# A stored instruction order for the second part of an attention and mixture-of-experts kernel, and two subtractions on another engine

## The chip, the cores and the metric

The kernel runs on one core of a Trainium2 chip. The metric is the device time of one execution in microseconds (us). A core has TensorE (PE: matmuls; PEld: its weight loads), VectorE (DVE), ScalarE (ACT), GpSimd (POOL) and SyncE (SP, which issues most DMAs). Each engine works through its own instructions in the order in which they stand in its queue, and waits on semaphores for the others.

## What is computed

Attention with four sink positions and a window of 128, and behind it a mixture of eight experts of which each token takes two. The random inputs are float32. Cut from the reference:

```python
keep = (pos[None, :] < 4) | ((rel >= 0) & (rel < 128))       # 4 batches, 8 heads, 768 positions, 64 wide
x = softmax(where(keep, q @ k.T / 8, -1e9)) @ v              # as 3072 tokens x 512
logits = x @ w_gate + log1p(exp(x @ w_noise)) * noise        # 3072 x 8
top2, top2_w = two largest of each row, softmax of the two
for e in range(8):
    for k in range(2):
        mask = top2[:, k] == e
        out[mask] += top2_w[mask, k, None] * (relu(x[mask] @ w1[e]) @ w2[e])   # 512 -> 1024 -> 512
```

## The kernel before

**Two parts.** The first part (to about 165 us of the profiled execution) is the attention, the routing of the first three batches and the start of expert 0; its order is a table, `ORDER`, carried out by `Plan.in_order`. The second part (`phase_two`) has the routing of the last batch and the experts. Both are written as a plan: `Plan.op` and `Plan.dma` record operations with an engine, a modelled duration, a priority and the keys that they read and write; nothing is issued until the plan is run. The second part is run by `Plan.run` (L1871: `p2.run()`), a list scheduler: at each step, of the operations that are ready on an engine by modelled times, it takes the one with the smallest priority. The order of each engine's queue follows from these model times. The constants of the model are `P2`.

**Routing of the last batch.** ScalarE and VectorE make the noisy logits, VectorE finds the two largest (L854, L858), their one-hot rows `oh` (L865) and their sum `m` (L867). TensorE ranks the tokens of each expert (`rank`, L875 to L881), VectorE makes factors from the ranks (L912 to L936; L936 multiplies last), TensorE places token numbers into the table of slots (`place`, L946), and VectorE makes the gather indices (`idg`, L970; `rt_idi`, L986). Indirect DMAs on GpSimd then fetch tokens: L1050 for the rest of expert 0, L1067 for the later experts, whose rows go by way of a DRAM buffer `x_sorted` (stores L1072, loads L1076 into `xg`, all issued by SP).

**Experts.** An expert has six or seven tiles of up to 128 tokens. Matrices are split into a high and a low half (`hi` on ScalarE, `lo` as a subtraction, L374 `minus`), and a product takes three matmuls. Expert 0 goes up (L1118 to L1120) and down (L1389 to L1391) in two pieces. Experts 1 to 7 go up by seven products of quarter matrices, named a to g, per pair of columns (L1519 to L1521, 6 matmuls each); several products add into the same accumulator bank, so ScalarE copies a bank out (`kept`, L1534) and VectorE adds (`added`, L1537) before the next product may write there; then ScalarE and VectorE make the two halves of the hidden rows (L1540, L1543). Each tile goes down by eight groups of three 512-column matmuls (a down product: L1550; the half tile L1553). ScalarE scales the sum (L1398), and GpSimd scatters it into the output with an adding indirect DMA (L1413). The last tile of all is added up on VectorE (L1431) to what a fetch brought, and stored (L1436).

**Buffers that tie the queues.** Weight chunks are loaded into two buffers `st` (L1181) and split from there (L1190, L1231, L374, L1239); rows into two `xg`, transposed on VectorE (L1273), which also takes the weights of the tokens from them (L1321, L1324), then split (L1287, L374); scaled sums have three buffers (laid in `turned` and `tmp`), each free when the scatter from it has landed; the banks of the products b and d have one buffer each.

**Two weight chunks of expert 0** (the last of w1, the third of w2; `w_chunk`, L1173) have their low half made by GpSimd:

```python
        if not q:
            w_chunk(plan, nc, c, sh, w1, w2, 0, 1, 3, -60, "Pool")
            w_chunk(plan, nc, c, sh, w1, w2, 0, 2, 2, -50, "Pool")
```

Of the kernel before, what the change touches and what calls it, by code (L numbers as in the profile page):

```python
# [76 lines left out]
)  # L77
ZERO = (0,) * 16
EACH = (0,) * 48
CAP = 832  # L80
# [5 lines left out]
ZEROS = 16  # L86
WIDE = 416
P2 = dict(sg=.01, ga=-57.86, gs=4.26, wt=-28.03, x=-83.35, xs=13.55, wa=-27.67, ws=27.26, w2=-33.31, w2s=11.84, wb=1.97,
          slack=0.55, sums=0.55, lands=3.2, late=0.93, gather=1.27, pair=5.89, a=1.92, b=7.67, d=7.57, c=-0.02,
          e=-5.07, f=-4.27, g=3.49)  # L90


# [4 lines left out]
PORT = 9  # L97
# [4 lines left out]
class Plan:  # L102
# [67 lines left out]
    def in_order(self, order, idle=None):  # L170


        n, ops = len(self.ops), self.ops
        left, succ = [len(o[4]) for o in ops], [[] for _ in ops]
        for i, o in enumerate(ops):
            for d in o[4]:
                succ[d].append(i)
        rows = {e: list(x) for e, x in order.items()}
        rows["DMA"] = [i + 1 for i in rows["SP"] if i + 1 < n and ops[i + 1][0] == "DMA"]
        assert sorted(sum(rows.values(), [])) == list(range(n))  # L180
        at, start, ptr = [self.low] * n, [0.0] * n, dict.fromkeys(rows, 0)
        free = {e: self.begin.get(e, self.low) for e in rows}
        kind, port = 0, self.low
        fill = []
        for _ in range(n):
            t, e = min((max(at[x[ptr[e]]], free[e], port if ops[x[ptr[e]]][6] == PORT else self.low), e)
                       for e, x in rows.items() if ptr[e] < len(x) and not left[x[ptr[e]]])
            i = rows[e][ptr[e]]
            ptr[e] += 1
            d = ops[i][1]  # L190
            if ops[i][6] == PORT:
                port = t + d
            start[i] = t
            if e == "PE":
                if idle and t < idle[0]:
                    w = max(free[e], idle[1])
                    fill += [w] * int((t - w) / (idle[2] * (2 if t < self.cold else 1)))
                d = (d + (SWITCH.get(kind, .1) if ops[i][6] != kind else 0)) * (2 if t < self.cold else 1)
                kind = ops[i][6]
            free[e] = end = t + d  # L200
            for s in succ[i]:
                lat = ops[i][5]
                if isinstance(lat, tuple):
                    lat = lat[e != ops[s][0]]
                if lat is None:
                    lat = SELF.get(e, .06) if e == ops[s][0] else self.LAT.get((e, ops[s][0]), .2)
                at[s] = max(at[s], end + lat)
                left[s] -= 1
        self.start, self.free = start, free
        for _, _, fn in sorted([(start[i], i, o[3]) for i, o in enumerate(ops) if o[3]] + [(t, -1, idle[3]) for t in fill], key=lambda x: x[:2]):  # L210
            fn()
        return max(free.values())
# [575 lines left out]
def routing(nc, plan, cst, sh, b, t0, nt, z, xbuf):  # L788
# [5 lines left out]
    last = T0 + nt == sh.T  # L794
    c, get = cst, plan.get
    gid = b
# [12 lines left out]
    def t(name):  # L809
        if name in ("oh", "z", "r2"):  # L810
            return (name, gid)
        if last and name in ys:
            return ("y", ys[name])
        if name == "lg":
            return ("lg", b)
        tag = "rt_" + name
        plan.rings.setdefault(tag, 1)
        return (tag, gid)
# [44 lines left out]
    pair = [128, 2, nt]  # L863
# [31 lines left out]
        for q in range(DM // 128):  # L895
            nc.sync.dma_start(dram(xbuf, (T0 + 1) * 128 * sh.XW + q * sh.SW + 128, [[sh.XW, 128], [128 * sh.XW, nt], [1, E]]), rt("w"))

    plan.dma(z if last else plan.now, keep, 1.2, r=[t("w")], w=[("wrow", gid)], u=[("old", 0)] * last, n=12)
    most = c["most"]
    ends = last or T0 + nt == sh.T - NT  # L900
    tab = lambda nm: c[nm].rearrange("p e t -> p (e t)")[:, fl]
    if ends:
        i = int(last)
# [137 lines left out]
def gather(plan, nc, cst, sh, xbuf, e, t, z, after=None):  # L1041


    n = sh.first[e] + t
# [8 lines left out]

    if not e:
        kept = [("xrow", n) for n in range(sh.NA // 256 * (sh.H // 2))] + [("wrow", b) for b in range(sh.B - 1)] + [("blank", 0)]
        plan.op("Pool", 1.28, z, go, r=[("idg", int(not first))] + kept * first, w=[row], lat=5.4 if first else 4)
        return
    m = n - sh.first[1]
    rows = cst["xsort"][m]
# [19 lines left out]
    if after:  # L1079
        key, src, region = after  # L1080
        held = [("held", n)]
        plan.op("Pool", .12, zs, lambda: nc.gpsimd.tensor_copy(cst["spacer"], src()), r=[key], w=held, u=[region], lat=0)  # L1082
    plan.op("Pool", P2["gather"], zs, sort, r=[("rt_idi", sh.B - 1)] + held + [("xe", f) for f in range(sh.F // 128)] * (m == 2), w=[sg], lat=P2["lands"])
    plan.dma(zs, store, 1.6, r=[sg], w=[("xs", n)], late=0)
    plan.dma(z, load, 1.4, r=[("xs", n)], w=[row], late=.5)

# [251 lines left out]
def experts(tc, plan, cst, sh, w1, w2, xbuf, out):  # L1338
# [122 lines left out]
    for q, (e, tiles, width) in enumerate(info):  # L1461
# [4 lines left out]
                weight(plan, nc, c, sh, e, t, -100 + (t - FA) * 7)  # L1466
                rows_turn(plan, nc, c, sh, e, t, size(e, t), "TX", -100 + (t - FA) * 7)
        if not q:
            w_chunk(plan, nc, c, sh, w1, w2, 0, 1, 3, -60, "Pool")
            w_chunk(plan, nc, c, sh, w1, w2, 0, 2, 2, -50, "Pool")  # L1470
        order = [t for t in tiles if size(e, t) == 128]
        order[1:1] = [t for t in tiles if size(e, t) != 128]
        for t in order:
# [334 lines left out]
def moe_kernel(ctx, tc, sh, qk_t, v, vsink, w_gates, noise, w1c, w2c, w1, w2, out):  # L1808
# [14 lines left out]
    with ExitStack() as both:  # L1823
# [44 lines left out]
        for i in range(int(late / .22)):  # L1868
            p2.op("PE", .22, -1000, lambda: ones(p2.get("Y", 0, [128, sh.DM], F32, "ps")))
        phase_two(tc, nc, p2, cst, sh, w1c, w2c, xbuf, out)  # L1870
        p2.run()  # L1871
    spill(tc, cst, sh, w1, w2, xbuf, out)


# [21 lines left out]
```

## Time and profile before

| | |
|---|---|
| Time, median of 3 runs | 717.66 us (717.14 to 718.05) |
| Time of the profiled execution | 718.88 us |
| Its span | 717.2 us, 13573 instructions |
| TensorE busy | 692.4 us (97%), 4755 matmuls |
| VectorE, ScalarE, GpSimd busy | 530.8 us (74%), 403.6 us (56%), 281.4 us (39%) |
| TensorE's granted clock | 0.9 or more of full in all 40 slices |
| Data moved by DMA | 123.41 MB, 172 GB/s on the mean |
| Chain that ended last, by engine | PE 74%, DMA 9%, DVE 5%, ACT 3%, issue 3%, POOL 3% |

The profile is that of one execution. Its span is what the instructions cover, its time has the start and end of the launch as well. The busy share says how much of the span an engine had an instruction in work; a matmul's end is modelled. An idle time in brackets in a row of the timeline is that of the engine just before that instruction, and behind the arrow stands what ended it. Lines are those of the kernel before.

### The profile page before, as it was taken

How to read it: one execution, taken by the hardware profiler on the slowest of the kernel's cores; microseconds unless marked ns; L12 is line 12 of the kernel's file. 1: busy time of each engine (PE TensorE's matmuls, PEld its weight loads, DVE VectorE, ACT ScalarE, POOL GpSimd, SP SyncE). 2: the span in 40 equal slices, each digit the busy share in tenths (PEclk: the TensorE clock that was granted, in tenths of full speed). 3: DMA queues.
4: the chain of work that ended last, by engine and by line, in shares of the span. 5: the costliest groups of instructions: out<-in, count | busy, mean ns of one | idle time of the engine just before them, and what ended most of it. 6: DMA issues, size and time to landing. Idle time of an engine off the chain costs nothing.

```text
span 717.2 us, 13573 instructions
## 1 busy us (share of the span) xinstructions
PE 692.4 (97%) x4755; PEld 586.5 (82%) x4755; DVE 530.8 (74%) x1279; ACT 403.6 (56%) x1115; POOL 281.4 (39%) x383
## 2 busy tenths in 40 slices
PE   8999999998999999998999999999999999999995
PEld 4777777766878889878988998898899889889984
DVE  7899988968526977957796769587877968775620
ACT  6998989763115545635564655355555555645430
POOL 3435575683227432552253316330732530181022
PEclk9999999999999999999999999999999999999999
DMA  7775787575479997566548655854576390264132
GB/s 252 218 259 163 240 272 200 139 200 183 153 244 228 319 286 232 103 156 197 177 95 205 172 153 131 209 161 140 129 229 201 90 253 32 89 121 100 59 45 46
DMA packets 87336, 123.41 MB, mean 172 GB/s; under 512 B 18656, under 2 KB 55392, under 8 KB 87264
## 3 DMA queue, kind: packets, MB, share of 16 engines
q1 hardware_dynamic: 75856, 94.64, 42.4%
q0 software_dynamic: 11408, 27.86, 19.4%
q8 instruction: 38, 0.62, 0.4%
q14 instruction: 34, 0.28, 0.1%
HBM read 81.75 MB, written 40.73 MB: 171 GB/s over the span
## 4 chain that ended last, share of the span: by engine, by line
PE 74%; DMA 9%; DVE 5%; ACT 3%; issue 3%; POOL 3%; SPq 0%; POOLq 0%; DVEq 0%; ACTq 0%
PE Y L1550 31%; PE B L1519 9%; PE B L1520 9%; PE B L1521 9%; PE S L468 3%; DMA xg<-x_sorted 3%; ACT cbuf L489 2%; DMA x_rows<-strip 2%; PE B L550 2%; DMA sg<-x_rows,idg 2%; PE Y L1553 2%; PE B L525 1%; DMA vn<-in_v 1%; PE B L553 1%; DMA xg<-x_rows,idg 1%
## 5 line engine op out<-in xcount | busy, mean ns | idle before, releaser
L1413 POOL DMA_INDIRECT out<-tmp,idx x34 | 87.1, 2562 | 153.3 <-ACT tmp L1398 149.1
L1520 PE MATMUL B<-x,wr 128*128 128x384 f32 (+1 forms) x392 | 134.7, 344 | 0.0
L1550 PE MATMUL Y<-w2a,hb 128*128 128x512 f32 x504 | 128.9, 395 | 0.0
L1550 PE MATMUL Y<-w2b,hb 128*128 128x512 f32 x504 | 124.8, 392 | 0.0
L1550 PEld LDWEIGHTS Y<-w2b,hb 128*128 128x128 f32 x504 | 94.5, 188 | 20.1
L1550 PEld LDWEIGHTS Y<-w2a,hb 128*128 128x128 f32 x504 | 94.2, 188 | 19.5
L1519 PE MATMUL B<-xe,wr 128*128 128x384 f32 (+1 forms) x224 | 77.2, 345 | 3.5 <-ACT tmp L1534 2.2
L1521 PE MATMUL B<-xe,wr 128*128 128x384 f32 (+1 forms) x224 | 76.8, 343 | 0.1
L1520 PEld LDWEIGHTS B<-x,wr 128*128 128x128 f32 x392 | 73.6, 188 | 2.5
L374 DVE TENSOR_TENSOR wr<-st,wr 128x512 fp32r<-128x512 f32 (+1 forms) x86 | 59.4, 695 | 13.3 <-ACT wr L1231 13.1
L489 ACT ACTIVATE cbuf<-S,nb 128x132 f32<-128x132 f32 x192 | 68.4, 372 | 0.9
L1231 ACT ACTIVATE wr<-st 128x512 fp32r<-128x512 f32 x84 | 52.2, 624 | 12.6 <-DVE st L374 9.8
L1519 PE MATMUL B<-x,wr 128*128 128x384 f32 (+1 forms) x168 | 57.9, 345 | 1.3 <-ACT tmp L1534 1.3
L1521 PE MATMUL B<-x,wr 128*128 128x384 f32 (+1 forms) x168 | 57.7, 343 | 0.9 <-DVE wr L374 0.9
L1082 POOL COPY spacer<-hb 1x1 f32<-1x1 f32 x38 | 12.3, 324 | 96.1 <-ACT hb L1540 88.2
L1519 PEld LDWEIGHTS B<-xe,wr 128*128 128x128 f32 x224 | 42.0, 188 | 7.3 <-ACT tmp L1534 3.1
L1398 ACT ACTIVATE tmp<-Y,wc 128x512 f32<-128x512 f32 x31 | 21.2, 688 | 46.8 <-PE Y L1550 32.7
L1413 POOL DMA_INDIRECT out<-turned,idx x17 | 31.9, 1876 | 36.9 <-ACT turned L1398 33.8
L1534 ACT ACTIVATE tmp<-B 128x384 f32<-128x384 f32 (+1 forms) x56 | 27.7, 499 | 32.3 <-PE B L1521 27.8
L1540 ACT ACTIVATE hb<-B 128x384 fp32r<-128x384 f32 (+1 forms) x56 | 28.0, 502 | 27.9 <-DVE B L1537 13.3
L468 PE MATMUL S<-kq 64*64 64x196 f32 (+2 forms) x768 | 40.9, 325 | 2.3 <-ACT cbuf L489 1.0
L1521 PEld LDWEIGHTS B<-xe,wr 128*128 128x128 f32 x224 | 42.0, 188 | 0.6 <-DVE wr L374 0.4
(314 smaller groups left out, 1553.6 us busy)
## 6 DMA issues: line engine op xcount, KB each, us to landing
st<-in_w1c SPq DMA_DIRECT2D x32, 512.0 KB
st<-in_w2c SPq DMA_DIRECT2D x32, 512.0 KB
kq<-in_qk_t SPq DMA_DIRECT2D x15, 780.0 KB
xg<-x_sorted SPq DMA_DIRECT2D x42, 272.0 KB
x_sorted<-sg SPq DMA_DIRECT2D x30, 272.0 KB
out<-zt SPq DMA_DIRECT2D x31, 256.0 KB
vn<-in_v SPq DMA_DIRECT2D x16, 384.0 KB
x_rows<-strip SPq DMA_DIRECT2D x48, 128.0 KB
```

Source lines behind the costliest of these rows:

```text
L374: eng.tensor_tensor(out, a, b, op=OP.subtract)
L468: nc.tensor.matmul(whole[x, h, c0:c1], kq(g)[r, KS + 128 * j + 64 * s:KS + 128 * j + 64 * s + 64], kq(g)[r, o + c0:o + c1], start=True, st ...
L489: nc.scalar.activation(C(n)[:, u], S_(n, 0, KW)[:, u // 2, u % 2], AF.Exp, scale=1.0 / math.sqrt(D), bias=get("nb", n)[:, u // 2, u % 2:u ...
L1231: plan.op("ACT", .03 + .255 * m, z, lambda: nc.scalar.activation(h(), src(), AF.Copy), r=[st], w=[(*key, b)] + old, u=[key, ex], lat=P2["s ...
L1398: nc.scalar.activation(get("y", Y[e, t], [128, DM]), get("Y", Y[e, t]), AF.Copy, scale=c["wc"][e % 2][:, t:t + 1])
L1413: d = nc.gpsimd.indirect_dma_start(out=out, out_offset=bass.IndirectOffsetOnAxis(ap=c["idx"][:size(e, t), e, t:t + 1], axis=0), in_=get("y ...
L1519: nc.tensor.matmul(p, wh, h, start=start and not k, stop=False, skip_group_check=True)
L1520: nc.tensor.matmul(p, wh, l, start=False, stop=False, skip_group_check=True)
L1521: nc.tensor.matmul(p, wl, h, start=False, stop=k == 1, skip_group_check=True)
L1534: nc.scalar.activation(u_of(e, k), src(), AF.Copy)
L1540: nc.scalar.activation(hx(e, f, 0, j), src(), AF.Relu)
L1550: nc.tensor.matmul(p, h[:, x * (CAP + R) + 128 * t:x * (CAP + R) + 128 * t + 128], w[:, y], start=(f == 0 and x + y == 0), stop=(f == FC - ...
```

## The change

The second part is no longer scheduled by `Plan.run`. A new table, `ORDER2`, holds for each engine the numbers of the plan's operations in the order in which they are to be issued, 688 for TensorE, 868 for VectorE and 520 for ScalarE, and `Plan.in_order` issues them so. The same operations are there, with the same tiles. `in_order` learns to place operations of the first part that the second reads (their engine is a tuple). The two subtractions of expert 0 go to VectorE. Some modelled times and reads change (a gather now names the rows of weights of the last batch among what it reads); the stored order, not these times, now sets each engine's queue.

```diff
+ORDER2 = dict(
+    PE=(15, 12, 13, 16, 11, 95, 96, 97, 14, 98, 103, 104, 105, 106, 33, 111, 112, 113, 114, 119, 163, 120, 121, 193,
...
-          slack=0.55, sums=0.55, lands=3.2, late=0.93, gather=1.27, pair=5.89, a=1.92, b=7.67, d=7.57, c=-0.02,
+          slack=0.25, sums=0.25, lands=3.2, late=0.93, gather=1.27, pair=5.89, a=1.92, b=7.67, d=7.57, c=-0.02,
...
+        rows.update({o[0]: [i] for i, o in enumerate(ops) if isinstance(o[0], tuple)})
...
-    plan.dma(z if last else plan.now, keep, 1.2, r=[t("w")], w=[("wrow", gid)], u=[("old", 0)] * last, n=12)
+    plan.dma(z if last else plan.now, keep, 1.2, r=[t("w")], w=[("wrow", gid)], u=[("old", 0)] * last, n=5 if last else 12)
...
-        plan.op("Pool", 1.28, z, go, r=[("idg", int(not first))] + kept * first, w=[row], lat=5.4 if first else 4)
+        plan.op("Pool", 1.28, z, go, r=[("idg", int(not first))] + (kept if first else [("wrow", sh.B - 1)]), w=[row], lat=5.4 if first else 4)
...
-        plan.op("Pool", .12, zs, lambda: nc.gpsimd.tensor_copy(cst["spacer"], src()), r=[key], w=held, u=[region], lat=0)
-    plan.op("Pool", P2["gather"], zs, sort, r=[("rt_idi", sh.B - 1)] + held + [("xe", f) for f in range(sh.F // 128)] * (m == 2), w=[sg], lat=P2["lands"])
+        plan.op("Pool", .7, zs, lambda: nc.gpsimd.tensor_copy(cst["spacer"], src()), r=[key], w=held, u=[region], lat=0)
+    plan.op("Pool", P2["gather"], zs, sort, r=[("rt_idi", sh.B - 1), ("wrow", sh.B - 1)] + held + [("xe", f) for f in range(sh.F // 128)] * (m == 2), w=[sg], lat=P2["lands"])
...
-            w_chunk(plan, nc, c, sh, w1, w2, 0, 1, 3, -60, "Pool")
-            w_chunk(plan, nc, c, sh, w1, w2, 0, 2, 2, -50, "Pool")
+            w_chunk(plan, nc, c, sh, w1, w2, 0, 1, 3, -60)
+            w_chunk(plan, nc, c, sh, w1, w2, 0, 2, 2, -50)
...
-        p2.run()
+        p2.in_order(ORDER2)
```

Three places show what moves. A row has the line, the operation, the tile written and, behind the arrow, those read. Lines of the changed kernel are 127 or 128 higher (L995 is L867 of before).

VectorE at the routing of the last batch, before: `m` is L867, `hb` the low half of expert 0's hidden rows, `oh` the one-hot rows.

```order
L854 MAX turned_152<-turned_152 128x8 x6
L1378 SCALAR_TENSOR_TENSOR hb_2996<-B2_78,hb_2996 128x512
L858 MAX_INDEX turned_152<-turned_152 128x8 x6
L865 TENSOR_TENSOR oh3_131<-io_94,turned_152 128x96
L888 RECIPROCAL z3_132<-turned_152 128x6
L867 TENSOR_TENSOR m_114<-oh3_131 128x48
L1378 SCALAR_TENSOR_TENSOR hb_2996<-B0_76,hb_2996 128x512
L912 COPY turned_152<-B3_79 128x8
```

The same place in the changed kernel:

```order
L982 MAX turned_152<-turned_152 128x8 x6
L986 MAX_INDEX turned_152<-turned_152 128x8 x6
L993 TENSOR_TENSOR oh3_131<-io_94,turned_152 128x96
L995 TENSOR_TENSOR m_114<-oh3_131 128x48
L1016 RECIPROCAL z3_132<-turned_152 128x6
L1506 SCALAR_TENSOR_TENSOR hb_3001<-B2_78,hb_3001 128x512
L1506 SCALAR_TENSOR_TENSOR hb_3001<-B0_76,hb_3001 128x512
L1045 TENSOR_TENSOR turned_152<-oh3_131,B3_79 128x96
```

The split of the hidden rows (L1378, now L1506) that stood between the maxima and their indices now stands behind `m`, beside the second one; `m` comes ahead of the reciprocal (L888, now L1016).

ScalarE around the first products of expert 2, before: L1190 splits weights, L1398 scales a sum for the scatter, the first L1534 copies out product a of expert 2.

```order
L1287 ACTIVATE x7_3455<-turned_152 128x4x32
L1287 ACTIVATE x7_3455<-turned_152 128x2x32
L1190 ACTIVATE w2a_4385<-st_4294 128x1024
L1398 ACTIVATE tmp_2956<-Y_4364,wc1_151 128x512
L1190 ACTIVATE w2a_4421<-st_4382 128x1024
L1534 ACTIVATE tmp_2956<-B2_78 128x416
L1540 ACTIVATE hb_2996<-B1_77 128x13x32
L1534 ACTIVATE tmp_2956<-B2_78 128x416
```

The same place in the changed kernel (L1526 scales, L1662 copies a product out, L1318 splits weights):

```order
L1526 ACTIVATE tmp_2956<-Y_3900,wc1_151 128x512
L1662 ACTIVATE tmp_2956<-B2_78 128x416
L1415 ACTIVATE xe_2923<-turned_152 128x4x128
L1318 ACTIVATE w2a_4383<-st_4328 128x1024
L1526 ACTIVATE turned_152<-Y_4214,wc1_151 128x512
L1662 ACTIVATE tmp_2956<-B2_78 128x416
L1662 ACTIVATE strip_153<-B2_78 128x416
L1318 ACTIVATE w2a_4435<-st_4371 128x1024
```

The first copy of a product stood behind both weight splits and a scaled sum; now it stands ahead of both weight splits, behind a scaled sum alone.

TensorE at its end, before: the last two tiles (two banks `Y`), each row two groups of three matmuls.

```order
L1550 MATMUL Y_7604<-w2a_7207,hb_2996 128x512 x6
L1550 MATMUL Y_7604<-w2a_7242,hb_2996 128x512 x6
L1550 MATMUL Y_7604<-w2b_7445,hb_2996 128x512 x6
L1550 MATMUL Y_7604<-w2b_7515,hb_2996 128x512 x6
L1550 MATMUL Y_7632<-w2a_7207,hb_2996 128x512 x6
L1550 MATMUL Y_7632<-w2a_7242,hb_2996 128x512 x6
L1550 MATMUL Y_7632<-w2b_7445,hb_2996 128x512 x6
L1550 MATMUL Y_7632<-w2b_7515,hb_2996 128x512 x6
```

The same place in the changed kernel: the last tile is Y_7603, Y_7586 the one before it, Y_7389 the one before that.

```order
L1678 MATMUL Y_7603<-w2a_7280,hb_3001 128x512 x3
L1678 MATMUL Y_7586<-w2a_7280,hb_3001 128x512 x3
L1678 MATMUL Y_7586<-w2b_7453,hb_3001 128x512 x6
L1678 MATMUL Y_7586<-w2b_7523,hb_3001 128x512 x6
L1678 MATMUL Y_7389<-w2b_7523,hb_3001 128x512 x6
L1678 MATMUL Y_7603<-w2a_7280,hb_3001 128x512 x3
L1678 MATMUL Y_7603<-w2b_7453,hb_3001 128x512 x6
L1678 MATMUL Y_7603<-w2b_7523,hb_3001 128x512 x6
```

Each tile went down in one run; now three tiles take turns, and the tile Y_7389 ends five groups of three before the end.

## Rows read from the trace of the kernel before

**Rows 1.** Busy time by stretches; columns: window, length, engines (instructions), clock, DMA.
```profile
340.00:360.00 20.00, 20.00 (x101) 18.65 (x100) 14.77 (x27) 11.96 (x23) 3.93 (x6) 1.00 0.61 185
```

**Rows 2.** Timeline of TensorE, its stops; columns: start, length, engine, line, operation [idle<-releaser].
```profile
173.98 0.18 PE L875 MATMUL B<-m,tri 128*128 128x48 bf16 x1 [1.45 <-DVE m L867]
...
199.67 0.43 PE L1145 MATMUL B<-idf,sg 64*128 64x64 f32 x4 [0.32 <-DMA sg<-x_rows,idg]
...
249.16 0.46 PE L1519 MATMUL B<-xe,wr 128*128 128x416 f32 x1 [1.28 <-DVE hb L1543]
...
255.22 0.45 PE L1521 MATMUL B<-x,wr 128*128 128x416 f32 x1 [0.86 <-DVE wr L374]
...
263.43 0.46 PE L1519 MATMUL B<-xe,wr 128*128 128x416 f32 x1 [0.24 <-ACT tmp L1534]
...
321.93 0.46 PE L1519 MATMUL B<-x,wr 128*128 128x416 f32 x1 [1.31 <-ACT tmp L1534]
...
326.47 0.45 PE L1519 MATMUL B<-xe,wr 128*128 128x416 f32 x1 [2.00 <-ACT tmp L1534]
```

**Rows 3.** Timeline of TensorE around the longest stop.
```profile
323.93 0.35 PE L1520 MATMUL B<-x,wr 128*128 128x416 f32 x1
...
324.12 0.34 PE L1521 MATMUL B<-xe,wr 128*128 128x416 f32 x1
...
326.76 0.35 PE L1520 MATMUL B<-x,wr 128*128 128x416 f32 x1
```

**Rows 4.** Timeline of GpSimd and VectorE at the routing of the last batch.
```profile
171.46 2.40 POOL L374 TENSOR_TENSOR hb<-st,hb 128x1024 fp32r<-128x1024 f32 x1 [0.72 <-ACT hb L1190]
...
171.66 2.27 DVE L867 TENSOR_TENSOR m<-oh 128x48 bf16<-128x48 f32 x1
...
175.15 1.25 DVE L1000 SCALAR_TENSOR_TENSOR turned<-turned,tie 128x8 f32<-128x8 f32 x1
...
193.16 1.23 DVE L374 TENSOR_TENSOR w2b<-st,w2b 128x1024 fp32r<-128x1024 f32 x1
```

**Rows 5.** Timeline of ScalarE and VectorE ahead of the last two stops.
```profile
314.12 0.69 ACT L1398 ACTIVATE tmp<-Y,wc 128x512 f32<-128x512 f32 x1 [7.00 <-DMA out<-tmp,idx]
...
320.41 1.06 ACT L1190 ACTIVATE w2a<-st 128x1024 fp32r<-128x1024 f32 x1 [2.42 <-DMA st<-in_w2c]
...
321.38 0.50 ACT L1534 ACTIVATE tmp<-B 128x416 f32<-128x416 f32 x1
...
323.06 0.71 DVE L1273 STREAM_TRANSPOSE turned<-xg 128x512 f32<-128x512 f32 x1 [3.28 <-DMA xg<-x_sorted]
...
324.80 0.59 DVE L1537 TENSOR_TENSOR B<-B,tmp 128x416 f32<-128x416 f32 x1
```

**Rows 6.** Timeline of VectorE from the rank to the first gathered tile.
```profile
174.91 0.17 DVE L912 COPY turned<-B 128x8 f32<-128x8 f32 x1 [0.38 <-PE B L881]
...
180.46 0.69 DVE L1378 SCALAR_TENSOR_TENSOR hb<-B,hb 128x512 fp32r<-128x512 f32 x1 [1.78 <-ACT hb L1370]
...
182.91 0.50 DVE L936 TENSOR_TENSOR tmp<-tmp,tok 128x336 f16<-128x336 f16 x1
...
185.93 0.14 DVE L970 TENSOR_TENSOR idg<-strip 128x3 int32<-128x3 f32 x1
...
192.26 0.15 DVE L1317 COPY wc<-sg 128x1 f32<-128x1 f32 x1 [3.30 <-DMA sg<-x_rows,idg]
```

**Rows 7.** Timeline of GpSimd at the end.
```profile
699.56 1.56 POOL L1413 DMA_INDIRECT out<-tmp,idx  x1 [4.01 <-ACT tmp L1398]
...
705.12 1.56 POOL L1413 DMA_INDIRECT out<-tmp,idx  x1 [3.97 <-ACT tmp L1398]
...
710.76 0.99 POOL L1436 DMA_INDIRECT out<-turned,idx  x1 [4.05 <-DVE turned L1431]
```

**Rows 8.** Busy time by stretches at the end (columns as in Rows 1).
```profile
707.00:710.00 3.00, 2.63 (x12) 1.83 (x10) 0.27 (x1) 0.00 (x0) 0.00 (x0) 1.00 0.74 93
...
712.00:714.00 2.00, 0.00 (x0) 0.00 (x0) 0.00 (x0) 0.00 (x0) 0.00 (x0) 1.00 0.36 135
```

More of the change, by code (lines that the diff above doesn't have):

```diff
@@ L77 @@
 )
+ORDER2 = dict(
+    PE=(15, 12, 13, 16, 11, 95, 96, 97, 14, 98, 103, 104, 105, 106, 33, 111, 112, 113, 114, 119, 163, 120, 121, 193,
[35 rows of a table added]
+    Pool=(17, 34, 36, 38, 39, 40, 203, 208, 73, 74, 213, 312, 76, 75, 320, 341, 348, 369, 376, 650, 659, 192, 397,
[7 rows of a table added]
+    DVE=(19, 22, 24, 23, 25, 26, 27, 28, 29, 30, 31, 32, 37, 100, 108, 47, 43, 48, 49, 52, 51, 18, 53, 61, 50, 62, 54,
[44 rows of a table added]
+    ACT=(20, 21, 99, 35, 107, 115, 89, 123, 206, 131, 93, 211, 139, 216, 147, 161, 155, 230, 222, 191, 329, 238, 246,
[26 rows of a table added]
+    SP=(87, 91, 101, 41, 109, 159, 133, 117, 762, 141, 125, 313, 417, 2355, 1739, 149, 418, 321, 157, 315, 342, 1431,
[8 rows of a table added]
+)
 ZERO = (0,) * 16
@@ L185, in in_order @@
         for _ in range(n):
-            t, e = min((max(at[x[ptr[e]]], free[e], port if ops[x[ptr[e]]][6] == PORT else self.low), e)
-                       for e, x in rows.items() if ptr[e] < len(x) and not left[x[ptr[e]]])
+            t, e = min(((max(at[x[ptr[e]]], free[e], port if ops[x[ptr[e]]][6] == PORT else self.low), e)
+                       for e, x in rows.items() if ptr[e] < len(x) and not left[x[ptr[e]]]), key=lambda x: (x[0], str(x[1])))
             i = rows[e][ptr[e]]
```

120 rows, old and new, of tables (ACT, DVE, PE, Pool) are left out of this document.

## The prediction

> **What bounds the kernel now.** I read the page's busy shares and slices first: TensorE leads everywhere. Then the table by stretches, which for a typical 20 us of the second part shows TensorE busy all 20.00 us, at a granted clock of 1.00 (the upper level, 2.4 GHz), while VectorE has 14.77 and ScalarE 11.96 [rows 1]. TensorE's work is the same set of instructions before and after, so the change can win only where TensorE stands still, and the second part has few such places. The timeline of TensorE shows every one: seven stops between 174 and 327 us, idle 1.45, 0.32, 1.28, 0.86, 0.24, 1.31 and 2.00 us, 7.46 us together [rows 2]. From there to the last matmul there is none. (The kernel's first part, up to about 165 us, keeps its stored order, and its idle time stays.)
>
> A stop costs more than its idle time, because the first matmul behind it runs alone. Two matmuls that follow each other start 0.19 us apart (323.93 and 324.12). Around the longest stop the starts are 324.12, 326.47, 326.76 [rows 2, 3]: 2.64 us for two steps that otherwise take 0.38, so 2.26 us lost with 2.00 idle, 0.26 more. Seven stops at 0.26 are 1.8 us, and 7.46 + 1.8 = 9.3 us is everything that a better order of the second part can give.
>
> **What ends the stops.** The first (rank, 173.98) waits for the table m from VectorE. That small operation lasted 2.27 us, 171.66 to 173.93, and GpSimd's 1024-wide subtraction ran from 171.46 to 173.86; a second small operation lasted 1.25 us as GpSimd's second subtraction ran [rows 4]. The Trainium skill (page "SBUF — State Buffer", section "Who interferes with whom") says that a VectorE operation with two inputs in SBUF and a GpSimd operation that reads SBUF hold one read port in turn, the second fully blocked. The trace agrees: m ended 0.07 us after the subtraction. If another cause held m, this stop would stay, and the sum below would be 1.7 us smaller; the two equal ends make me take it as gone.
>
> The others have one pattern: an in-order queue of VectorE or ScalarE has, ahead of the operation that TensorE wants, one that waits for a landing. Before 321.93 ScalarE had stood 7.00 us for a scatter whose buffer it needs (to 314.12) and 2.42 us for a weight load (to 320.41), and only then copied the product out (321.38). Before 326.47 VectorE had stood 3.28 us for rows (to 323.06), then split weights, and the sum that TensorE's bank needs came at 324.80 [rows 2, 5]. The stops from 249 to 263 have ScalarE and VectorE full of splits for the first of the later experts; that at 199.67 waits for a gather itself.
>
> **The change part by part.** *Two subtractions to VectorE.* GpSimd loses 2.40 us twice, VectorE gains about 1.23 us twice (its own subtraction of that size [rows 4]). The order puts one behind the routing tables and one later, among splits, each ahead of the TensorE work that reads it by many operations; the cover is VectorE's idle time there (3.30 us before 192.26 alone [rows 6]). Cost on the path: nothing; if the cover were gone, 1.2 us each.
>
> *The order.* In the queue of ScalarE the copy of expert 2's first product now stands ahead of both weight splits and of the scaled copies that waited for scatters; VectorE's sum for it stands ahead of the row transposes; the products and the remaining down products are interleaved, so that more TensorE work lies between a product and the next that needs its bank. That is the counter-measure to each of the six stops, and I take all as gone: +9.3 us. The queues of SP and GpSimd are rearranged too: gathers for the first expert's last tiles and the sorted rows come earlier, the rows of the tiles after next are read later, so a late landing has more time.
>
> *What is late next.* (a) The table placement on TensorE. A down product, three 512-column matmuls, takes 0.7 us: the eight of one tile lie between two scatters, 699.56 and 705.12 [rows 7]. Between rank and placement the new order has nine groups of that size, about 6.2 us. VectorE's part from the rank's counts to the last factor took 174.91 to 183.41 before, 8.5 us; of these 1.1 were blocked (1.25 against some 0.15), 1.8 idle and 0.6 a split for an expert [rows 4, 6], which leaves 5.0. With four small operations moved in between (0.1 each) and a split of 0.6 put ahead, it is 6.0: just in time. Each late hand-over counts in full, so 0 to 0.8; I take 0.3. (b) The first gathered tile. The index was made at 185.93, the row usable at 192.26: 6.3 us [rows 6]. In the new order eleven groups of 0.7, 7.7 us, lie on TensorE between the placement and the turn of that tile, and on VectorE a part of the moved subtraction (1.2) and a few small operations ahead of the index, 1.2 to 1.7 us: again just in time. Stop of 0 to 1.0; I take 0.2. (c) The tail. The tile before the last now ends five down products before the end, not eight: its scatter is issued 3 x 0.7 = 2.1 us later, 707.2 instead of 705.12. Its transfer, which before filled 707 to 710 (DMA share 0.74), now follows another scatter's, to about 713; the last store, issued at 710.76, moved its data from 712 to 714 [rows 7, 8]. The end moves by 0 (transfers side by side) to 0.9 us; I take 0.5, the middle. The Trainium skill's page "DMA: Bandwidth & Descriptors", section "Two DMAs through the same engine are not ordered", says that descriptors of one queue start in order: by it the tail costs 0.9, and the time would be 0.4 us above my forecast; no row here separates the two. (d) New stops in the 360 us that had none: with every queue rearranged I allow one of the smallest kind, 0.24 + 0.26 = 0.5; bounds 0 and the rivals below.
>
> **Sum.** 9.3 - 0.3 - 0.2 - 0.5 - 0.5 = 7.8 us. The profiled execution took 718.88 us (span 717.2 and 1.7 around it), 1.2 more than the median of the timed runs, 717.66; 7.8 less is 711.1 for the former and 709.9 for the median, which I forecast.
>
> **Rivals.** *Half of it comes back.* The landings that made the stops are not under the order's control: the 7.00 us wait hangs on a scatter. If the stops only move to other places, as each queue is still in order, 4 to 5 us come back: about 714. For: five stops within 80 us show how easily it happens. Against: the old order ran the last 390 us without one, though its queues have such waits there too.
>
> *The turnovers become stops (slower).* Place: the seven changes from one expert to the next. The new order starts an expert's first products some four to five down products earlier, so its split rows and weights have about 3 us less. If they aren't there, TensorE stops at every turnover. At the price of the longest stop (2.26 us) seven are 15.8 us: 717.66 - 9.3 + 15.8 + 0.9, about 725. It decides from 9.3 / 7 = 1.3 us a turnover. For: ScalarE and VectorE were behind TensorE at the first two turnovers [rows 2]. Against: the splits are reordered too, those that the first products read first, and the rows are asked for earlier.
>
> *No change.* TensorE's stops are set by what lands, not by the order, or the stored order is not better: 716.3 to 719.
>
> **How the numbers follow.** Forecast case (stops gone, 707.8 to 712.5): 0.70. Half back (712.5 to 716.2): 0.16. Within 0.2% (716.2 to 719.1; about what a measurement of this kernel can tell from no change): 0.07. Slower, about 725: 0.07. The lower end is 717.66 - 9.3 = 708.4, less some 0.6 for hold-ups too short to be listed as idle, 707.8; the upper end, 714.2, takes in half of the second case, so that about 0.2 is left outside. Faster 0.86, same 0.07, slower 0.07.
>
> **What would show it.** In the profile after: rank's row without idle before it, and m at about 0.2 us; no row of TensorE with over 0.5 us idle between 165 and 700 us, above all none near the first products of experts 1 and 2; the last store issued about 7.3 us earlier than 710.76, and at most 0.9 us more from there to the end than before. Wrong would be: idle time of 1 us or more at each turnover, behind ScalarE's or VectorE's splits, or a stop before the placement longer than 1 us, or m still long.

## The result and the profile after

The changed kernel took 710.31 us (median of 4, 708.59 to 711.34), the kernel before in the same comparison 717.4 us: a ratio of 0.990 (95% interval 0.988 to 0.993), 7.1 us less. In two later comparisons it took 709.58 and 709.36 us, with ratios of 0.989 (0.987 to 0.991) and 0.988 (0.985 to 0.990). The forecast was 709.9.

The page of its profile (span; busy time and share by engine; engines of the chain that ended last):

```profile
span 709.6 us, 13548 instructions
...
PE 691.3 (97%) x4755; PEld 588.3 (83%) x4755; DVE 527.5 (74%) x1281; ACT 398.1 (56%) x1115; POOL 252.3 (36%) x381
...
PE 86%; POOL 3%; DMA 3%; ACT 3%; DVE 2%; issue 2%; SPq 0%; POOLq 0%; DVEq 0%; ACTq 0%
```

TensorE's busy time is that of before within 1.1 us; what went is the time in which it stood. Its share of the chain of work that ended last rose from 74% to 86%. In the order of the stops of before [rows 2], the timeline of TensorE after (start, length, engine, line, operation, idle time and what ended it):

```profile
163.40 0.63 PE L1273 MATMUL B<-idf,xg 128*128 128x128 f32 x4 [1.45 <-DMA xg<-x_rows,idg]
...
173.47 0.20 PE L1003 MATMUL B<-m,tri 128*128 128x48 bf16 x1
...
180.50 0.33 PE L1074 MATMUL B<-strip,tmp 128*128 128x56 f16 x6
...
188.92 0.66 PE L1273 MATMUL B<-idf,sg 128*128 128x128 f32 x4 [0.24 <-DMA sg<-x_rows,idg]
```

The ranks (173.47) and the table placement (180.50) start without idle time. The turn (the transposing by matmuls) of the first gathered tile waited 0.24 us, and that is the only stop over 0.15 us from 165 us to the last matmul; there is none at the first products of experts 1 and 2. The row at 163.40 belongs to the first part, whose order is unchanged.

VectorE's timeline in the same stretch:

```profile
171.41 0.21 DVE L995 TENSOR_TENSOR m<-oh 128x48 bf16<-128x48 f32 x1
...
174.30 0.69 DVE L1506 SCALAR_TENSOR_TENSOR hb<-B,hb 128x512 fp32r<-128x512 f32 x1 [1.36 <-ACT hb L1498]
...
179.77 0.50 DVE L1064 TENSOR_TENSOR tmp<-tmp,tok 128x336 f16<-128x336 f16 x1
...
180.29 1.22 DVE L502 TENSOR_TENSOR hb<-st,hb 128x1024 fp32r<-128x1024 f32 x1
...
182.01 0.15 DVE L1098 TENSOR_TENSOR idg<-tmp 128x3 int32<-128x3 f32 x1
```

`m` lasts 0.21 us where it lasted 2.27 [rows 4]. The factors are done at 180.27, and the first subtraction fills VectorE behind them. The gather index follows at 182.01, 3.9 us earlier than before, when it stood at 185.93 [rows 6].

ScalarE at the first products of expert 2, where it had waited 7.00 and 2.42 us for landings [rows 5]:

```profile
312.39 0.52 ACT L1662 ACTIVATE tmp<-B 128x416 f32<-128x416 f32 x1 [0.74 <-PE B L1649]
...
313.33 1.05 ACT L1318 ACTIVATE w2a<-st 128x1024 fp32r<-128x1024 f32 x1
...
316.74 0.52 ACT L1662 ACTIVATE tmp<-B 128x416 f32<-128x416 f32 x1 [1.13 <-PE B L1649]
```

Both copies of products (L1662) now wait for TensorE, 0.74 and 1.13 us, instead of the other way round, and the weight split between them (313.33) finds its data loaded. This is so along the whole second part. ScalarE's and VectorE's waits for DMA landings (the arrival of a transfer's data) between 165 and 705 us, before (what waits, for what: us in total, times, longest):

```profile
ACT tmp L1398 <- DMA out<-tmp,idx: 13.8, 5, 7.0
...
ACT w2a L1190 <- DMA st<-in_w2c: 5.0, 3, 2.4
...
ACT wr L1231 <- DMA st<-in_w1c: 2.8, 2, 1.7
...
ACT turned L1398 <- DMA out<-turned,idx: 2.2, 2, 1.3
...
DVE turned L1273 <- DMA xg<-x_sorted: 9.8, 7, 3.3
...
DVE wc L1317 <- DMA sg<-x_rows,idg: 3.5, 2, 3.3
...
DVE strip L1321 <- DMA xg<-x_sorted: 2.5, 3, 1.1
```

And after:

```profile
ACT tmp L1526 <- DMA out<-tmp,idx: 3.5, 3, 1.7
...
ACT wr L1359 <- DMA st<-in_w1c: 2.2, 2, 1.8
...
ACT turned L1526 <- DMA out<-turned,idx: 0.8, 2, 0.5
...
ACT w2a L1318 <- DMA st<-in_w2c: 0.2, 1, 0.2
...
DVE wc L1445 <- DMA sg<-x_rows,idg: 3.7, 1, 3.7
```

39.6 us have become 10.4, and VectorE does not wait for sorted rows at all.

Some of the lateness of the landings lies on GpSimd, which issues the scatters. The 7.00 us [rows 5] were a wait for this one of the kernel before:

```profile
305.69 5.13 POOL L1413 DMA_INDIRECT out<-tmp,idx  x1 [0.27 <-DVE turned L1273]
```

It lasted 5.13 us on GpSimd, the next one (at 315.08) 1.57. Of the 52 scatters 14 lasted over 2.4 us in this profile, and as many in those of e1 and e5; in the changed kernel and in e6 it was 3. What held them was not tested, nor how much of the shorter landing waits comes from it. Expert 2's two stops went in e5 with these scatters as they were.

The end of the kernel, GpSimd's last row and the busy time of a stretch (columns as in [rows 1]):

```profile
703.16 0.99 POOL L1564 DMA_INDIRECT out<-turned,idx  x1 [1.41 <-DVE turned L1559]
```

```profile
702.00:704.00 2.00, 0.03 (x1) 0.00 (x0) 0.75 (x1) 0.00 (x0) 0.84 (x1) 1.00 0.97 125
```

The last store is issued at 703.16, 7.60 us earlier than before [rows 7], and from there to the end of the span it takes 6.4 us, as before, though the DMA engines have a share of 0.97 there. (In the seven other profiles with this tail it takes 6.4 to 7.1 us.)

One thing in this execution is not of the order. Busy time by stretches behind the late row at 163.40:

```profile
165.00:168.00 3.00, 3.00 (x9) 1.65 (x8) 2.44 (x6) 0.62 (x2) 0.00 (x0) 0.50 0.79 250
...
170.00:173.00 3.00, 3.00 (x14) 2.46 (x14) 2.42 (x20) 0.69 (x2) 1.04 (x4) 1.00 0.62 225
```

The granted clock was 0.50 (the lower level, 1.2 GHz) from about 164.9 to 168.3 us, and 9 matmuls fitted into 3 us where 14 did later. Two more profiles of the same kernel don't have it.

To compare executions without the first part, whose length varies (the second starts between 163.2 and 165.3 us), I take from each profile the time from the turn of the first part's last row tile on TensorE (before: 164.28) to the start of VectorE's last operation (709.73). Each such number is of one execution.

| Kernel | Time, median (us) | Second part (us) |
|---|---|---|
| before | 717.4, 717.55, 717.2, 718.09 | 545.45 |
| changed (three comparisons) | 710.31, 709.58, 709.36 | 537.60, 536.21, 536.47 |
| e1 subtractions alone | 717.29 | 546.55 |
| e2 three moves | 718.03 | 545.99 |
| e5 seven moves | 714.87 | 541.95 |
| e3, e9 changed order, subtractions back | 710.53, 710.55 | 537.41, 537.38 |
| e4 old front, new rest | 709.89 | 536.38 |
| e6 old front untouched, new rest | 711.33 | 538.19 |
| e7 changed, warm and later | 709.38 | 535.92 |

### The profile page after: what moved, and what is told of

The parts are those of the page before. It is cut to its first block, busy times and chain, and to the rows that moved or that the text cites. A ratio compares the mean times of both kernels' runs of the same rounds, so it can differ in the third digit from the quotient of the medians.

```text
span 709.6 us, 13548 instructions
## 1 busy us (share of the span) xinstructions
PE 691.3 (97%) x4755; PEld 588.3 (83%) x4755; DVE 527.5 (74%) x1281; ACT 398.1 (56%) x1115; POOL 252.3 (36%) x381
## 4 chain that ended last, share of the span: by engine, by line
PE 86%; POOL 3%; DMA 3%; ACT 3%; DVE 2%; issue 2%; SPq 0%; POOLq 0%; DVEq 0%; ACTq 0%
PE Y L1678 32%; PE B L1648 10%; PE B L1647 10%; PE B L1649 10%; PE S L596 4%; PE B L678 2%; PE B L653 2%; ACT cbuf L617 2%; PE Y L1681 2%; PE B L681 2%; PE Y L1519 1%; PE Y L1517 1%; PE Y L1518 1%; PE B L1246 1%; PE B L708 1%
## 5 line engine op out<-in xcount | busy, mean ns | idle before, releaser
L1678 PE MATMUL Y<-w2a,hb 128*128 128x512 f32 x504 | 131.7, 395 | 0.0
L1678 PE MATMUL Y<-w2b,hb 128*128 128x512 f32 x504 | 126.9, 392 | 0.0
L1541 POOL DMA_INDIRECT out<-tmp,idx x34 | 62.2, 1830 | 133.3 <-ACT tmp L1526 116.7
L1662 ACT ACTIVATE tmp<-B 128x384 f32<-128x384 f32 (+1 forms) x56 | 28.0, 500 | 55.9 <-PE B L1649 49.0
L1195 POOL DMA_INDIRECT sg<-x_rows,rt_idi x30 | 34.0, 1134 | 64.2 <-DMA x_sorted<-sg 48.2
L1665 DVE TENSOR_TENSOR strip<-B,strip 128x384 f32<-128x384 f32 (+1 forms) x28 | 16.0, 570 | 44.1 <-PE B L1649 23.7
L1526 ACT ACTIVATE tmp<-Y,wc 128x512 f32<-128x512 f32 x31 | 21.2, 686 | 38.7 <-PE Y L1678 33.2
```

The source lines that it names most:

```text
L1195: nc.gpsimd.indirect_dma_start(out=stage(), out_offset=None, in_=xbuf, in_offset=bass.IndirectOffsetOnAxis(ap=cst["idw"]()[:, sh.TE * e + ...
L1526: nc.scalar.activation(get("y", Y[e, t], [128, DM]), get("Y", Y[e, t]), AF.Copy, scale=c["wc"][e % 2][:, t:t + 1])
L1541: d = nc.gpsimd.indirect_dma_start(out=out, out_offset=bass.IndirectOffsetOnAxis(ap=c["idx"][:size(e, t), e, t:t + 1], axis=0), in_=get("y ...
L1662: nc.scalar.activation(u_of(e, k), src(), AF.Copy)
L1678: nc.tensor.matmul(p, h[:, x * (CAP + R) + 128 * t:x * (CAP + R) + 128 * t + 128], w[:, y], start=(f == 0 and x + y == 0), stop=(f == FC - ...
```

## The experiments

### The subtractions alone (e1)

The old order, written down as a table, with the two subtractions (operations 90 and 94) moved to VectorE:

```diff
-    Pool=(17, 34, 36, 90, 38, 94, 39, 40, 73,
+    Pool=(17, 34, 36, 38, 39, 40, 73,
...
-    DVE= 54, 55, 116, 56,
+    DVE= 54, 55, 90, 116, 56,
...
-    DVE= 84, 86, 204, 132,
+    DVE= 84, 86, 94, 204, 132,
```

> The old order, stored as a table, with one part of the change alone: the two subtractions of expert 0 on VectorE, the first put into its idle time of 1.78 us before 180.46, the second into that of 3.30 us before 192.26. Theory (GpSimd's subtraction holds m): m lasts about 0.2 us instead of 2.27, the stop of 1.45 us before rank goes, the six other stops stay as they are: 1.7 us less than the kernel before. Rival 1 (m is held by something else): m and the stop stay, time the same. Rival 2 (the later stops hang on what lands, and not on where TensorE stands): m is short and the first stop goes, but the stops from 249 us on grow by 1.7 us together, time the same.

717.29 us against 717.55, ratio 0.9987 (0.9966 to 1.0008): the interval holds both 1.7 us and nothing. The timelines of VectorE (first row) and TensorE say more:

```profile
172.64 0.21 DVE L997 TENSOR_TENSOR m<-oh 128x48 bf16<-128x48 f32 x1
...
173.35 0.20 PE L1005 MATMUL B<-m,tri 128*128 128x48 bf16 x1
...
249.45 0.46 PE L1649 MATMUL B<-xe,wr 128*128 128x416 f32 x1 [1.80 <-DVE hb L1673]
...
256.62 0.46 PE L1651 MATMUL B<-x,wr 128*128 128x416 f32 x1 [1.98 <-DVE wr L504]
```

`m` is short and the stop before the ranks is gone, so it was the subtraction that held it. But the next two stops are longer here than in [rows 2]: 1.80 for 1.28, and 1.98 for 0.86. Of the last three, that at 263 us is gone, and those of expert 2 are 1.16 and 1.86 for 1.31 and 2.00; from 249 us on it is 6.80 us together for 5.69. Behind the stop of 1.98 the clock fell (granted clock, the last column but two):

```profile
259.00:261.00 2.00, 2.00 (x7) 1.89 (x7) 0.59 (x1) 1.15 (x2) 0.99 (x1) 0.50 1.02 383
```

It was at 0.50 from about 258.1 to 261.5 us. One profile can't tell whether these two stops grew because TensorE came earlier (rival 2) or by chance: in the profiles of e2 and e5 that at 249 us is 1.16 and 1.67, and that at 255 absent and 0.79, with the same order ahead of them. The worth of the subtractions was therefore measured where the rest is quiet, in e4, e6 and e9.

### Three moves, then seven, in the old order (e2, e5)

```diff
-    ACT=  815, 648, 819, 792, 795, 798,
+    ACT=  815, 648, 792, 819, 798, 795,
...
-    DVE=  1032, 1033, 1043, 820, 794, 1040, 1041,
+    DVE=  1032, 1033, 794, 1043, 820, 1040, 1041,
```

792 and 798 copy products out, 819 splits weights, 794 adds, 1043 transposes rows.

> The old order, stored, with three operations moved at expert 2 and nothing else: ScalarE copies the first product out ahead of the weight split that waited 2.42 us for its load, and the second product ahead of the hidden rows; VectorE adds up the first product ahead of the row transpose that waited 3.28 us. Theory (a queue had an operation that waits for a landing ahead of the one that TensorE wants): the stops of 1.31 and 2.00 us go, 3.8 us less with their first matmuls, the other five stay. Rival (the landings themselves set the pace): TensorE stops a little later for the split rows or weights, and most of the 3.8 us come back; time within 1 us of the kernel before.

718.03 us, ratio 0.9999 (0.9977 to 1.0021): nothing gained. TensorE shows why:

```profile
327.33 0.72 PE L1649 MATMUL B<-x,wr 128*128 128x416 f32 x1 [2.73 <-DVE strip L1667]
...
327.84 0.55 PE L1650 MATMUL B<-x,wr 128*128 128x416 f32 x1
...
328.19 0.55 PE L1651 MATMUL B<-x,wr 128*128 128x416 f32 x1
```

The two stops are gone, and one of 2.73 us stands behind them. VectorE at that moment:

```profile
326.36 0.19 DVE L1451 TENSOR_TENSOR strip<-xg,pick 128x32 f32<-128x32 f32 x1 [3.20 <-DMA xg<-x_sorted]
...
326.69 0.58 DVE L1667 TENSOR_TENSOR strip<-B,strip 128x416 f32<-128x416 f32 x1
```

The operation in front of the sum that TensorE wanted takes token weights from the next row tile, and waited 3.20 us for it: the next one in the queue that hangs on a landing. And this stop cost more than its length: matmuls that start 0.19 us apart at the upper clock [rows 3] started 0.35 apart, with the granted clock at 0.50 from about 326.7 to 333.5 us:

```profile
328.00:333.00 5.00, 5.00 (x16) 4.82 (x15) 4.02 (x10) 2.52 (x6) 1.52 (x2) 0.50 0.19 58
```

From 327.33 to 333.65 there are 18 starts: 6.3 us for what takes 3.4 at 0.19, so 2.9 us lost beside the stop itself. e5 also moves the four operations on the next two row tiles (1062 and 1063, 1070 and 1071) behind the sums:

```diff
-    DVE=  796, 1062, 1063, 802, 804, 808, 1070, 809, 1071, 824, 811, 838, 825, 826, 840,
+    DVE=  796, 802, 804, 808, 809, 1062, 1063, 824, 811, 838, 825, 826, 840, 1070, 1071,
```

> The kernel with three moves at expert 2, and four more: VectorE takes the token weights of the next two row tiles (for which it stood 3.20 us, with the sum that TensorE wanted behind them) six and three operations later. Theory (every operation that waits for a landing has to stand behind what TensorE wants soon, and three moves left one out): no stop between 318 and 335 us, no fall of the clock there, 3.8 us less than the kernel before. Rival (the rows land later for it, since their buffer is freed later, and the stop goes on to the next one): another stop of over 1 us before 345 us, time within 1.5 us of the kernel before.

714.87 us against 717.2, ratio 0.9965 (0.9951 to 0.9979): 2.3 us less, and 3.5 less in the second part of the profiled execution. TensorE has no idle time at expert 2, at full clock:

```profile
318.00:345.00 27.00, 27.00 (x141) 25.98 (x140) 21.85 (x48) 15.89 (x33) 9.03 (x13) 1.00 0.74 230
```

The theory's 3.8 us were nearly met in the profile, where the stops that were left alone happened to be 0.6 us longer than in [rows 2]; the medians show less. So it is the position in the queue that makes the stop, and one operation left in the wrong place is enough to get it back. The times of e5 also vary less (714.3 to 715.7) than those of the kernel before beside it (715.5 to 720.5).

### The subtractions back on GpSimd in the new order (e3, e9)

```diff
-    DVE=  59, 656, 90, 77, 78,
+    DVE=  59, 656, 77, 78,
...
-    DVE=  72, 94, 68, 132,
+    DVE=  72, 68, 132,
...
-    Pool=(17, 34, 36, 38, 39, 40, 203, 208, 73, 74, 213, 312,
+    Pool=(17, 34, 36, 38, 39, 40, 90, 203, 208, 73, 74, 213, 94, 312,
```

> The changed kernel's order with the other part undone: the two subtractions are GpSimd's again, the first as soon as its high half is there (ScalarE ends that at 178.8 us in the changed kernel), the second behind the third gather. Theory (it is the subtraction beside VectorE's operations that costs): VectorE's factors after 178.9 us wait about 2.1 us, the table placement on TensorE, which has no slack, stops about 2 us, and with 1.2 us less for VectorE to do ahead of the index the stop of 0.24 us at the first gathered tile goes: 1.5 to 2.4 us more than the changed kernel. Rival (the stored order alone does it, the engine of the subtractions doesn't matter): the same time as the changed kernel, or up to 0.5 us less.

710.53 us, ratio 0.9889 (0.9856 to 0.9922), which alone looked like the rival. GpSimd (first row), VectorE and TensorE:

```profile
177.14 3.70 POOL L504 TENSOR_TENSOR hb<-st,hb 128x1024 fp32r<-128x1024 f32 x1 [4.95 <-ACT hb L1320]
...
178.05 0.50 DVE L1066 TENSOR_TENSOR tmp<-tmp,tok 128x336 f16<-128x336 f16 x1
...
178.47 2.42 DVE L1458 TENSOR_TENSOR pick<-own,perm 128x32 f32<-128x32 f32 x1
...
188.29 0.66 PE L1275 MATMUL B<-idf,sg 128*128 128x128 f32 x4 [1.32 <-DMA sg<-x_rows,idg]
```

VectorE's factors were not held: the operations up to 178.05 kept their 0.50 us, and it was the subtraction that got stuck, 3.70 us long instead of 2.40. But the next one, an operation of 32 elements, then took 2.42 us, as `m` had. It stands ahead of the index and not of the placement, so the stop came at the first gathered tile, 1.32 us, and not before the placement. To measure its size the same kernel ran again beside the changed one.

> The changed order with the subtractions on GpSimd, this time beside the changed kernel itself on one chip. By the traces it loses a stop of 1.32 us (1.1 to 1.6 us with the first matmul) at the first gathered tile, since VectorE's small operation ahead of the index waits 2.42 us for the subtraction: 1.1 to 1.6 us above the changed kernel. Rival (the times of the two calls, 710.5 and 709.6 us, differ by the chip only): within 0.4 us of it.

> The changed kernel, as the reference for the one with the subtractions back: about 709.6 us, no stop over 0.3 us from 165 us to the end.

710.55 us (709.74 to 711.92) against 709.36 (708.56 to 710.21) on the same chip: 1.2 us. The profile has the operation at 2.42 us again and a stop of 1.28 us; the changed kernel beside it had one of 0.38, a little over what was expected of it. This is within the 1.1 to 1.6 us expected here, though the times of the two kernels overlap slightly. The theory of e3 stands, with the place wrong and the size below its range of 1.5 to 2.4.

### The old front with the new rest (e4, e6)

The queues up to about 212 us in the old order (232 of the plan's operations), all others in the changed kernel's; e4 has the subtractions on VectorE as in e1, e6 on GpSimd as before:

```diff
+front = operations that the old order starts up to 212 us
+ORDER2[engine] = [i for i in old[engine] if i in front] + [i for i in new[engine] if i not in front]
```

> The old order up to about 212 us (the routing of the last batch and most of expert 0), with the subtractions moved as in the kernel that moves them alone, and the changed kernel's order from there on. Theory (the new order of the experts takes their five stops away by itself): none of the stops from 249 to 327 us, that of 0.32 us before 199.67 still there; 1.7 + 7.0 = 8.7 us less than the kernel before. Rival (the experts' stops hang on how early the gathers of the routing are issued): two or more of the five stay, at most 5 us less.

709.89 us, ratio 0.9879 (0.9846 to 0.9911). None of the five stops of the experts is there. The only one from 165 us on is at the seam of the two orders:

```profile
215.27 0.39 PE L1248 MATMUL B<-hb,wr 128*128 128x320 f32 x1 [0.51 <-DVE strip L1451]
```

The stop of 0.32 us at 199.67 wasn't there in this execution, one of those that come and go. So the five stops go with the new order of the experts, whatever stands ahead of them. The new order of the front adds nothing that shows: the changed kernel took 709.36 to 710.31 us in other comparisons. Within the experts' order, e4 does not separate the queues of ScalarE and VectorE from those that issue the transfers, SyncE's and GpSimd's.

> The old order up to about 212 us with the subtractions left on GpSimd, and the changed kernel's order from there on: against the kernel with the old front and moved subtractions (709.9 us) it differs by the two subtractions alone. Theory (TensorE is dense behind, so a stop can't be caught up): the stop of 1.45 us before rank is there again and costs 1.7 us: 711.6 us. Rival (the two subtractions' engine doesn't matter for the time, as in the changed order): 709.9 us.

711.33 us, ratio 0.9917 (0.9901 to 0.9934), 1.4 us more than e4 (of an earlier comparison) and 1.8 in the second part:

```profile
172.88 0.18 PE L1005 MATMUL B<-m,tri 128*128 128x48 bf16 x1 [1.44 <-DVE m L997]
```

The stop before the ranks is there, and with a dense TensorE behind it nothing catches it up. The theory's 1.7 us hold. None of the experts' five stops is there, so their order alone makes 5.9 us (717.2 less 711.33).

### The changed kernel again, and its last stop (a_again, e7)

> The changed kernel once more, as the reference for the others of this call: about 710.3 us. If the granted clock of 0.50 from 164.9 to 168.2 us, which its first profile shows behind the late rows at 163.40, was chance, this profile has it not, and its span is about 1.3 us shorter; if it belongs to the order, it is there again.

709.58 us (709.19 to 710.14). No fall of the clock from 160 us to the last matmul (there was one in the first part, from 12.3 to 15.8 us) and no stop from 165 us on, not even that of 0.24; the second part is 1.4 us shorter than in the first profile.

```diff
-    PE= 194, 205, 165, 185,
+    PE= 194, 165, 205, 185,
...
         o, x = get(ring, ti, [128, c, 128], F32, "ps"), get(*row)
+        for _ in range(6 if not e and t == 2 else 2 if not e and t == 3 else 0):
+            nc.tensor.matmul(o, cst["one"], cst["one"][:, None, :].to_broadcast([128, 4, 128]), start=True, stop=True)
```

> The changed kernel with its last stop attacked, and the fall of the clock: the turn of the first gathered tile stands one group of three matmuls later on TensorE, and eight matmuls without use stand in the waits for the first part's last rows (six ahead of the one at 163.40, two ahead of the one at 164.54). Theory: the stop of 0.24 us goes (0.5 us with its first matmul), and the clock stays at 1.00 from 160 to 170 us in every execution, which is 1.3 us in those that had it fall: 0.5 to 1.3 us less than the changed kernel. Rival: the extra matmuls hold up the turns where the rows are there early, and eat what is gained: the same time.

709.38 us (708.47 to 709.55) against 709.58: 0.2 us, within what varies. TensorE over the first part's last waits:

```profile
160.00:166.00 6.00, 5.45 (x40) 3.39 (x32) 4.47 (x13) 2.66 (x5) 0.00 (x0) 1.00 1.03 365
```

It is busy 5.45 of 6 us there and the clock stays up; no stop is left from 165 us on. The gain is below the 0.5 us that the theory had at the least. No turn is seen to be held up, which speaks against the rival's reason, but its time is the one measured: the run does not decide. The changed kernel's second and third profiles had no fall of the clock there either, so this one doesn't show that the added matmuls prevented one. What there is to gain behind the change is, by estimate, a few tenths and, in an execution like the first profiled one, about 1 us (537.60 against 536.21 and 536.47 in the second part).

### Rows that land late (e8)

```diff
-        nc.sync.dma_start(x, rows.rearrange("q (s i) d -> (q s) (i d)", i=4)[:, :size // 32 * sh.SW])
+        for _ in range(2):
+            nc.sync.dma_start(x, rows.rearrange("q (s i) d -> (q s) (i d)", i=4)[:, :size // 32 * sh.SW])
```

> The kernel before, with each load of sorted rows (41 of them) issued twice into the same buffer; the second waits for the first, which took a median of 4.2 us in the changed kernel, so every row tile lands about 4 us later, and SyncE's queue stands that long each time. Theory (the old order's stops come from operations that wait for a landing ahead of what TensorE wants, so its time hangs on the landings): stops in many more places, one of 1 to 3 us for most of the seven experts, 8 us or more above the kernel before (over 725 us). Rival (the rows land with time to spare in either order): within 2 us of the kernel before.

> The same second load of each row tile in the changed kernel. Theory (the new order keeps what waits for a landing behind what TensorE wants soon, and asks for rows earlier, so it takes later landings): at most 3 us above the changed kernel's 709.6, few stops of over 0.5 us; the distance to the kernel before with the same load grows. Rival (its queues are as tight, only tuned to these landings): it loses as much as the kernel before does, 8 us or more.

800.05 us, ratio 1.113 (1.109 to 1.117), for the kernel before, which took 718.57 beside it: 81 us lost. 745.85 us, ratio 1.038 (1.034 to 1.042) for the changed one: 36 us lost. (The ratio is to the kernel before without second loads, the 36 us are against the changed kernel's 709.6.) Both lose far more than was expected, so the sizes were wrong; the theory's order of the two holds, and neither rival does. The loads also hold up SyncE, so weights land late as well. Some of the longest waits, of TensorE, VectorE and ScalarE, in the kernel before:

```profile
PE B L1520 <- ACT tmp L1535: 30.1, 8, 7.9
...
DVE turned L1274 <- DMA xg<-x_sorted: 71.7, 25, 5.8
...
DVE strip L1322 <- DMA xg<-x_sorted: 40.6, 18, 4.7
...
ACT w2a L1191 <- DMA st<-in_w2c: 44.9, 6, 9.0
```

And in the changed kernel:

```profile
PE Y L1682 <- ACT hb L1657: 6.6, 2, 4.1
...
DVE turned L1402 <- DMA xg<-x_sorted: 17.6, 10, 3.3
...
DVE strip L1450 <- DMA xg<-x_sorted: 15.0, 7, 3.7
...
ACT wr L1360 <- DMA st<-in_w1c: 25.6, 9, 6.4
```

TensorE's wait for copies of products in the old order (30 us in eight stops) is the old pattern, now at most changes of expert; VectorE waits 112 us for rows. In the new order it waits 33 us for the same rows, and the largest stops are of another kind: the hidden rows come late. The new order has more time in hand for a landing and loses less than half as much, but it isn't free of them.

## Why the prediction was right

**The stops and their sum.** +9.3 us was taken for seven stops. The 0.26 us beside the idle time come out of the rows at the five stops of the experts; at the two short matmuls (173.98, 199.67) it was about 0.15, so the stops of that profile are worth 9.1 us. The second part went from 545.45 us to 537.60, 536.21 and 536.47 in the changed kernel's three profiles: 7.9 (with the fall of the clock), 9.2 and 9.0. The pattern that I read from [rows 2, 5], a queue with an operation ahead that waits for a landing, is shown for expert 2's two stops by e2 and e5. The three stops from 249 to 263 us went with the experts' order (e4, e6); which operations of it made them was not tested. e4 and e6 divide the gain: the experts' order carries most, the subtractions 1.4 to 1.8 in the old front and 1.2 in the new order.

**What held m.** Right (e1, e6), and seen a second time on another operation (e3, e9).

**The charges.** They were mostly not there. The placement: I counted 6.0 us on VectorE against 6.2 on TensorE. VectorE took 6.0, from the split put ahead (174.30) to the last factor (180.27); TensorE had more between, 7.0 us from the ranks (173.47) to the placement (180.50): 0 for 0.3. The first gathered tile: idle 0.24, 0 and 0.38 us in three profiles, with about 0.15 more each where it is there, for 0.2: right. New stops: none for 0.5. The tail: from VectorE's last operation to the end 7.43, 7.73 and 7.69 us against 7.48 before, so 0 to 0.2 for 0.5; in five more profiles with this tail (e3, e4, e6, e7, e9) 7.45 to 8.17. By what the Trainium skill's page "DMA: Bandwidth & Descriptors", section "Two DMAs through the same engine are not ordered", says of the order in which descriptors start, I had made it 0.9; the DMA share from 702 to 704 us was 0.97, and the end moved by 0.7 us at the most.

**From the trace to the time.** Of the charges of 1.5 us some 0.4 came (0.3 at the first gathered tile and 0.1 at the tail, on the mean of the three profiles). With the stops at 9.1 us the gain should have been 8.7 us, not 7.8, and in the second part it was 8.7 on the mean. The times show 7.1, 7.6 and 8.7. So the step from one profile to the medians gave back what the charges overstated: the profiled execution of before was 1.2 us slower than the median, and I took the whole worth of its stops off the median. That the two errors are of one size, and the forecast so close, is luck; the stops and what ends them are not. The kernel before runs from 715.2 to 723.5 us, and its stops differ from one execution to the next (e1, e2, e5); how much of the missing 0 to 1.6 us is that, and how much the clock's falls, stays open.

**The price of a stop.** Idle time and 0.26 us held for the experts' stops of [rows 2], none of which had the clock fall. It is a lower bound: the stop of 2.73 us in e2 cost about twice its length. That e2 gained nothing is the rival "half of it comes back" in small: with few operations moved, the stop moves on.

**The other rivals.** The turnovers have no stop; under late rows the old order stops there up to 7.9 us, the new one nowhere over 4.1. "No change" is excluded by the interval.

## What to carry to other kernels

When the busiest engine stops, look in the queue of the engine that it waits for, at what stands ahead of the wanted operation: if that hangs on a transfer, move it back, and then all others like it, since the next one takes its place. Read a stop's worth from a stretch in which the clock did not fall, and judge small edits where the rest of the program is quiet: the same two subtractions were lost in the spread of the old order and plain at 1.2 to 1.8 us with the experts' new one. An order that leaves time for late landings can also make the times vary less: here from 708.6 to 711.3 us in all runs of the changed kernel, and from 715.2 to 723.5 before.

## What the runs showed of the hardware

Small VectorE operations beside a GpSimd subtraction ended with it: `m`, 2.27 us [rows 4], the one of 1.25 us in the same rows (175.15 to 176.40, the second subtraction 173.98 to 176.37), and that of 2.42 us in e3 and e9. In e3 it was first the other way: the subtraction started at 177.14 while VectorE worked without a gap up to 178.5, and lasted 3.70 us instead of 2.40. So in these runs the one that came second waited. The Trainium skill, page "SBUF — State Buffer", section "Who interferes with whom", says that issue order decides who blocks; the trace agrees.

The clock fell to 0.50 in a stop of 2.73 us (e2), behind two of 1.80 and 1.98 us that lay 7 us apart (e1) and behind waits of 1.45 and 0.51 us in the changed kernel's first profile, and it did not fall behind the one of 2.00 us in [rows 2], where one of 1.31 us lay 4.5 us ahead. In the kernel before with the rows loaded twice it did not fall behind stops of 3.42 us (273.50) and 3.21 us (287.11) either. The length of a stop alone did not tell which it would be.
